# Two memory chains worked by halves of the heads, in a set TensorE order, with full row tiles for the last 64 channels

## The chip, the cores and the metric

The kernel runs on one core of one Trainium2 chip. The metric is the device time of one execution in microseconds (us). The page of a profile names the engines PE (TensorE), PEld (TensorE's weight loads), DVE (VectorE), ACT (ScalarE), POOL (GpSimd) and SP (SyncE).

## The reference, cut to what matters

The output is a gate between two attention layers, and the kernel returns it with the gradients of eleven inputs. The change touches layer B alone, which carries a memory of 8 tokens through 64 segments of 32 tokens, with 32 heads of 128:

```python
mem = mem0                                    # 8 x 576
for s in range(64):
    h = concatenate([mem, x[32*s : 32*s+32]]) # 40 tokens
    q, k, v = h @ Wq, h @ Wk, h @ Wv          # 32 heads x 128
    p = softmax(q k^T * scale + mask)
    o = (p v) @ Wo
    mem = o[:8]                               # into the next segment
    outs.append(o[8:])
```

The kernel does what depends on x alone in bulk, and only the 8 memory tokens in order: a forward chain of 64 segments, and for the gradients a backward chain from the last segment to the first. Each segment waits for the one before.

## The kernel before

The 8 x 576 memory is held as columns: four blocks of 128 channels and one of 64 (`NKT` = 5). A projection is five row blocks times four groups of four heads; the groups stand side by side in the array (`tp`), so four matmuls of 512 columns run at once. The fifth block has 64 rows only. One segment of the forward chain:

```python
S = psum.tile([P, 512], F32, name="c_S", bufs=1)
self.mm(S[:, :], lhsT=self.identB[:, :], rhs=self.maskC..., start=True, stop=False)
for wi, w in enumerate("qkv"):
    for r in range(2):                        # halves of the heads
        for kt in range(NKT):
            for g in range(4):
                wap, rows = self.w_nat(w, kt, c * 512, (c + 1) * 512)   # 64 rows where kt == 4
                self.mm(pb[32 * g:32 * g + 32, :], lhsT=mT[rows, kt, s * MEM:s * MEM + 32],
                        rhs=wap, start=(kt == 0), stop=(kt == NKT - 1), tp=(rows.start, 32 * g))
        self.evac(tm[w][:, r, :], pb[:, :])
    ...                                       # 8 transposes, one copy for all heads
...                                           # 16 score matmuls
self.busy(pf, 2, mE[:, 0:512])
nc.scalar.activation(ET[:, :], S[:, :], ACT.Exp, scale=SCALEB)     # all heads at once
...                                           # row sums, outputs
self.busy(pf, 4, ET[:, :])
...                                           # reciprocal, scaling, two transposes
self.busy(pf, 4, oc[:]...)
...                                           # 96 matmuls with Wo
self.rows_to_columns(...)                     # the result to columns: the tail
```

`busy` is a fill-in matmul: its result goes nowhere, and it is there to keep TensorE's clock up.

```python
def busy(self, pf, n, rhs):
    for _ in range(n):
        self.mm(pf[0:32, 0:w], lhsT=self.identB[:, 0:32], rhs=rhs)
```

The backward segment begins with the probabilities, computed again:

```python
nc.scalar.activation(ET[:, 256:512], S[:, :], ACT.Exp, scale=SCALEB)
for x in range(2):
    self.mm(Sg[:, 1, :], lhsT=self.onesPB[:, :], rhs=ET[:, 256 * x:256 * x + 256], ...)
nc.vector.reciprocal(rlb[:, :], Sg[:, 1, :])  # 128 x 256
self.evac(cc[:], pt[:])                       # q, k and probabilities, transposed
...                                           # dO = gradient @ Wo^T, 40 matmuls
self.busy(self.pf, 2, dO[:, 0]); self.busy(self.pf, 1, dO[:, 1])
...                                           # dO^T, dP, dS, each for all heads
project(3, "v", ...); project(2, "k"); project(1, "q")   # 288 matmuls into one accumulator
self.rows_to_columns(...)
```

## Time and profile before

| | us |
|---|---|
| median of 3 runs | 9754.34 |
| up to the first forward copy | 3997 |
| forward chain, 62 segments | 1112 |
| between the chains | 1639 |
| backward chain, 63 segments | 1149 |
| after it | 1842 |

The chain rows run from the first to the last of the copies that end a segment (`c_mT`, `d_gT`); their lines and those of single segments are in the prediction below. The period between two such copies is the measure: it repeats 62 and 63 times in one trace.

### The profile page before, as it was taken

Reading aid. Unit: us, or ns where it says so; the run is one execution under the profiler, and the core shown is the slowest. Engines: PE = TensorE matmul, PEld = TensorE weight load, DVE = VectorE, ACT = ScalarE, POOL = GpSimd, SP = SyncE. Lnnn points to the kernel's source line nnn. Section 1 sums busy time; section 2 is a strip of 40 time slices with the busy share of each in tenths; the row PEclk is TensorE's granted clock in tenths of the full one; section 3 lists DMA queues with packets and bytes.
Section 4 is the critical chain, followed back from the end, with each engine's and each line's share of the span. In section 5 each row is a group of like instructions: output and inputs, shape, how many; then the busy total and the mean of one; then the engine's idle time right before and its main releaser. Section 6 shows DMA issues by size and latency. Waiting matters only on the chain. (4 is left out here: it accounts for less than half of the span.)

```text
span 9738.9 us, 211095 instructions
## 1 busy us (share of the span) xinstructions
PE 9052.5 (93%) x91222; PEld 4192.6 (43%) x91222; DVE 4369.3 (45%) x6082; ACT 3748.2 (38%) x6962; POOL 1261.4 (13%) x2887
## 2 busy tenths in 40 slices
PE   7999999999999898899998888887999989998899
PEld 2222222222223344445455555554666655554444
DVE  4889888889887343122223333332222211113100
ACT  3878778778876233111113222221111111112000
POOL 3000000000000233000002222221000001112000
PEclk9999999999999899899997777777999987776999
DMA  2000000000000555211115444444222256666444
GB/s 80 1 5 5 1 5 5 1 5 5 1 1 27 211 232 214 88 48 51 48 49 196 155 157 156 155 161 164 77 78 80 77 176 185 190 186 210 166 150 145
DMA packets 550264, 961.40 MB, mean 99 GB/s; under 512 B 183433, under 2 KB 361746, under 8 KB 529170
## 3 DMA queue, kind: packets, MB, share of 16 engines
q1 hardware_dynamic: 484002, 697.41, 22.3%
q0 software_dynamic: 64016, 249.18, 6.7%
q8 instruction: 713, 11.68, 0.5%
q14 instruction: 221, 1.81, 0.1%
q10 hardware_dynamic: 1312, 1.33, 0.0%
HBM read 543.67 MB, written 404.03 MB: 97 GB/s over the span
## 5 line engine op out<-in xcount | busy, mean ns | idle before, releaser
L1128 DVE TENSOR_TENSOR a_U<-a_d,a_E 128x1024 bf16<-128x1024 f32 x2048 | 2472.6, 1223 | 295.2 <-ACT a_E L1123 224.0
L1123 ACT ACTIVATE a_E<-a_s 128x512 bf16<-128x512 f32 x4096 | 2237.7, 595 | 556.7 <-PE a_s L78 471.8
L78 PE MATMUL a_s<-a_qaug,a_kmask 128*128 128x512 bf16 x2048 | 700.1, 385 | 54.7 <-ACT a_tk L1205 24.5
L78 PE MATMUL a_s<-a_kmask,a_qaug 128*128 128x512 bf16 x2048 | 697.1, 383 | 25.9 <-ACT a_E L1123 9.6
L78 PE MATMUL w_acc<-w_col,w_h 128*128 128x512 bf16 (+1 forms) x2400 | 525.5, 380 | 11.0 <-DMA w_col<-dqx 11.0
L78 PEld LDWEIGHTS <-d_g 128*32 128x32 bf16 x18432 | 498.9, 97 | 26.2 <-DVE d_g L740 9.8
L62 DVE CAST p_tok<-p_pb 128x512 bf16<-128x512 f32 x384 | 265.2, 691 | 319.1 <-PE p_pb L78 319.1
L78 PE MATMUL a_d<-a_doT,a_vaugT 32*128 32x512 bf16 x2048 | 399.0, 386 | 0.0
L78 PE MATMUL a_d<-a_vaugT,a_doaT 32*128 32x512 bf16 x2048 | 398.0, 385 | 0.0
L78 PEld LDWEIGHTS <-w_h 128*128 128x128 bf16 (+1 forms) x2400 | 237.3, 100 | 299.4 <-issue 33.7
L64 ACT COPY p_em<-p_tr 128x512 bf16<-128x512 bf16 x384 | 224.7, 585 | 358.7 <-PE p_tr L83 358.5
L1215 POOL TENSOR_TENSOR a_otok<-a_tk,a_rl 128x144 bf16<-128x144 f32 x64 | 27.4, 428 | 2514.1 <-DVE a_rl L1214 2514.1
L78 PEld LDWEIGHTS <-a_vaugT 32*128 32x128 bf16 x2048 | 96.1, 91 | 569.0 <-issue 569.0
L78 PEld LDWEIGHTS <-a_doaT 32*128 32x128 bf16 x2048 | 96.3, 91 | 537.9 <-issue 537.5
L64 ACT CAST c_tm<-c_pb 128x512 bf16<-128x512 f32 x192 | 112.3, 585 | 540.7 <-PE c_pb L78 540.7
L78 PEld LDWEIGHTS <-c_mT 128*32 128x32 bf16 (+1 forms) x7680 | 166.7, 94 | 328.9 <-issue 209.6
L824 ACT ACTIVATE g_dt<-x_p 128x512 bf16<-128x512 f32 x256 | 142.7, 600 | 355.2 <-DMA dvx<-g_dt 185.4
L62 DVE CAST w_o<-w_acc 128x512 bf16<-128x512 f32 (+1 forms) x60 | 41.4, 690 | 491.7 <-PE w_acc L78 475.4
L78 PEld LDWEIGHTS <-a_kmask 128*128 128x128 bf16 x2048 | 124.9, 97 | 311.2 <-issue 303.1
L78 PEld LDWEIGHTS <-p_xT 128*128 128x128 bf16 (+1 forms) x1920 | 155.0, 97 | 218.4 <-issue 88.4
L345 DVE CAST d_ws<-d_pw 96x128 bf16<-96x128 f32 x64 | 18.4, 287 | 497.9 <-ACT d_ws L344 497.9
L78 PE MATMUL x_b<-WTq,g_dqe 128*128 128x512 bf16 (+1 forms) x1024 | 200.7, 360 | 42.9 <-DMA g_dqe<-dqe 42.9
(485 smaller groups left out, 15029.5 us busy)
## 6 DMA issues: line engine op xcount, KB each, us to landing
xt_k<-p_tok SPq DMA_DIRECT2D x16, 1024.0 KB, 3.9
xe_k<-p_em POOLq DMA_DIRECT2D x16, 1024.0 KB, 5.3
xs_k<-p_seg POOLq DMA_DIRECT2D x64, 256.0 KB, 3.6
xt_v<-p_tok SPq DMA_DIRECT2D x16, 1024.0 KB, 4.0
xe_v<-p_em POOLq DMA_DIRECT2D x16, 1024.0 KB, 5.8
xs_v<-p_seg POOLq DMA_DIRECT2D x64, 256.0 KB, 3.7
xt_q<-p_tok SPq DMA_DIRECT2D x16, 1024.0 KB, 4.2
xe_q<-p_em POOLq DMA_DIRECT2D x16, 1024.0 KB, 5.8
```

Source lines behind the costliest of these rows:

```text
L62: nc.vector.tensor_copy(out, in_)
L64: nc.scalar.copy(out, in_)
L78: self.follow(self.nc.tensor.matmul(out, lhsT, rhs, start=start, stop=stop, tile_position=tp, skip_group_check=True))
L345: nc.vector.tensor_copy(ws[0:96, 0:128], pw[0:96, 0:128])
L824: nc.scalar.mul(dt[:, g], pk[:], sc)
L1123: nc.scalar.activation(ex[:, j, :], s[:, :], ACT.Exp, scale=SCALEA)
L1128: nc.vector.tensor_tensor(out=u[:], in0=d[:], in1=ex[:], op=ALU.mult)
L1215: nc.gpsimd.tensor_tensor(out=osl, in0=v[:, :, :, o0:o0 + DA], in1=rl[:].to_broadcast([P, 4, 2, DA]), op=ALU.mult)
```

## The change

Its intent is to shorten a segment in three ways: full 128-row tiles (zeros beside the last 64 channels), so that TensorE never changes to the 64-row shape; every step between projections done for 16 heads at a time, so that VectorE and ScalarE work on one half while TensorE works on the other; and an order for TensorE written out by hand and held (`chain`), with useful work where fill-in matmuls stood. The 1/sum of the softmax is also kept from the forward chain, and a backward segment needs eight matmuls fewer besides the fill-in ones: two row sums, and six of those that build dP. Cut to its core:

```diff
-        mT = keep.tile([P, NKT, NSEG * MEM + 32], BF16, name="c_mT")
+        mT = keep.tile([P, NKT + 1, NSEG * MEM + 32], BF16, name="c_mT")
+        self.chain = True
...
+                        elif w == "v":
+                            blk, rhs = 4 + r, self.Wv5[:, g * 512:(g + 1) * 512]
+                        else:
+                            blk, rhs = 4 + (w == "k"), self.Wqk5[:, c * 512:(c + 1) * 512]
+                        self.mm(pb[32 * g:32 * g + 32, :], lhsT=mT[:, blk, s * MEM:s * MEM + 32], rhs=rhs,
+                                start=(kt == 0), stop=(kt == NKT - 1), tp=(0, 32 * g))
...
+            project("q", 0, "v")
+            project("q", 1, "s")
+            project("k", 0, "v")
             for r in range(2):
+                self.evac(half(0, r), compact(columns("q", r)), use="vs"[r])
+            project("k", 1, "s")
+            project("v", 0, "v")
...                                           # k transposes
+            project("v", 1, "s", 0)           # three of its five row blocks
...                                           # mask and scores
+            for r in range(2):
+                nc.scalar.activation(ET[:, :, rs], S[:, :, rs], ACT.Exp, scale=SCALEB)
+            project("v", 1, "s", 1)           # the other two, while ScalarE works
-            self.busy(pf, 4, ET[:, :])
-            self.busy(pf, 4, oc[:].rearrange("p r n -> p (r n)"))
+            output(0)
...
+            self.busy(pf, 1, ET[:, 0, :])
+            output(1)
+            out_columns(0)
...
+            out_project(0, 8)
+            out_columns(1)
+            out_project(8, 32)
...                                           # backward
+            rlb = L["rlb"] = sp.tile([P, 256], F32, name="d_rlb", bufs=2)
+            nc.sync.dma_start(rlb[:, :], self.RL_m[s].partition_broadcast(P))
-            nc.vector.reciprocal(rlb[:, :], Sg[:, 1, :])
+            def weight_gradients(r):
+                dP[r] = psum.tile([P, 2, P], F32, name="d_S", bufs=1)
...
+            gradient_rows(0)
+            own_exps(L)
+            gradient_rows(1)
+            gradient_columns(0)
+            fill(1, dO[0][:, 0:192])
+            gradient_columns(1)
+            compact_gradient(0)
+            weight_gradients(0)
+            compact_gradient(1)
+            score_gradients(0)
...
+            project(3, "v", 16, 32)
+            project(2, "k", 0, 32)
+            project(1, "q", 0, 32)
+            if nxt:
+                own_scores(nxt)               # of the next segment, under the tail
```

## The prediction

> **What bounds the kernel now.** I read the page first, then stretches of 100 us with the granted clock, then the two chains instruction by instruction.
>
> ```profile
> PE 9052.5 (93%) x91222; PEld 4192.6 (43%) x91222; DVE 4369.3 (45%) x6082; ACT 3748.2 (38%) x6962; POOL 1261.4 (13%) x2887
> PE   7999999999999898899998888887999989998899
> PEclk9999999999999899899997777777999987776999
> ...
> 4500.00:4600.00 100.00, 99.67 (x1652) 49.31 (x1644) 23.59 (x55) 19.93 (x39) 3.00 (x11) 1.00 0.15 45
> 7300.00:7400.00 100.00, 98.56 (x2249) 69.79 (x2251) 28.69 (x59) 14.18 (x35) 0.62 (x5) 1.00 0.27 85
> ...
> L352 DVE CAST c_mT<-c_tr x63: 198/200/201, 3997.4 to 5109.5; 128x40 bf16<-128x40 f32 x63
> L352 DVE CAST d_gT<-d_tr x64: 198/199/200, 6748.5 to 7897.0; 128x40 bf16<-128x40 f32 x64
> ```
>
> TensorE is busy everywhere (first number of a stretch), the others below half. The last two lines are the copies that end one segment of the forward and of the backward memory chain. So the forward chain takes (5109.5 - 3997.4)/62 = 17.94 us a segment, the backward one (7897.0 - 6748.5)/63 = 18.23 us, together some 2,320 of 9,754 us. A segment needs the one before it, so each microsecond of one counts 63 or 64 times. The 99% busy there mean little: part is filler, and matmuls overlap. One forward segment, in order of time:
>
> ```profile
> 4499.79 1.05 PE L78 MATMUL c_pb<-Wq,c_mT 128*32 128x512 bf16 x16
> 4500.77 0.40 PE L78 MATMUL c_pb<-Wqk,c_mT 64*32 64x512 bf16 x4
> 4501.09 1.05 PE L78 MATMUL c_pb<-Wq,c_mT 128*32 128x512 bf16 x16
> 4502.07 0.40 PE L78 MATMUL c_pb<-Wqk,c_mT 64*32 64x512 bf16 x4
> 4502.40 0.40 PE L83 MATMUL c_tr<-identB,c_tm 128*128 128x128 bf16 x4
> 4502.73 0.60 PE L78 MATMUL c_pb<-Wk,c_mT 128*32 128x512 bf16 x5
> ...
> 4513.30 2.82 PE L78 MATMUL c_S<-Wo,c_mE 128*32 128x192 bf16 x96
> 4515.95 0.59 PE L78 MATMUL c_pf<-c_mE,identB 128*32 128x512 bf16 x2
> 4516.16 0.21 ACT L344 CAST c_ws<-c_S 96x64 bf16<-96x64 f32 x1 [4.76 <-PE c_S L78]
> 4516.40 0.29 DVE L345 CAST c_ws<-c_S 96x128 bf16<-96x128 f32 x1 [3.16 <-ACT c_ws L344]
> 4517.47 0.20 DVE L352 CAST c_mT<-c_tr 128x40 bf16<-128x40 f32 x1 [0.78 <-PE c_tr L78]
> ```
>
> and the start of a backward one:
>
> ```profile
> 7314.69 1.76 DVE L669 RECIPROCAL d_rlb<-d_g 128x256 f32<-128x256 f32 x1 [1.09 <-PE d_g L78]
> 7316.37 0.50 DVE L62 COPY d_cc<-d_tr 128x768 bf16<-128x768 bf16 x1
> 7316.78 0.68 DVE L62 CAST d_dO<-d_pb 128x512 bf16<-128x512 f32 x1
> 7317.51 0.81 PE L78 MATMUL d_pf<-d_dO,identB 128*32 128x512 bf16 x3 [0.31 <-DVE d_dO L62]
> ```
>
> Four matmuls of 32 columns by 512 run side by side, so 16 are four groups. Starts tell the cost: the 16 take 0.98 us to the next kind, the 4 with 64 rows 0.32. At 0.216 us a group that is 0.11 us over, at each change of tile shape; 4 transposes take 0.33 = 4 x 0.056 + 0.11. In the backward piece the reciprocal and the copy behind it hold VectorE until the cast of dO starts late, and TensorE waits.
>
> **What the Trainium skill says.** "TensorEngine Tiling (Array Packing)", Key Properties: changing the tiling mode drains TensorE. The trace agrees, 0.11 us each. "TensorE: Matmul & The Clock Gate", "Wait - 56ns, not 53.3ns?": 215.7 ns for 512 columns, 55.6 for 128; the groups above agree. Same page, Part 1: the clock is judged in free-running windows of 3.41 us and is full or half. The clock records agree: lengths are multiples of 3.41, values 1.0 or 0.5. I summed streamed columns (at the page's 2.4 GHz, half in the low state) per such window over the whole trace: every drop followed a window that streamed at most 45% of the time; none followed a fuller one. "PSUM - Partial Sum Buffer", bank collisions: accesses by two engines to one bank are kept apart. In the tail above, ScalarE's cast ends at 4516.37 and VectorE's begins at 4516.40.
>
> **The change, forward.** Drain 0.11, group of 512 0.216, transpose 0.056, all from above. Before, 4499.79 to 4517.72: projections with their transposes up to the scores 10.01; scores to the first output matmul 1.45; outputs to Wo 2.05; Wo 2.57; tail 1.85; sum 17.93.
>
> After: (1) The last 64 channels become full 128-row tiles (zeros beside them), so the 64-row shape is gone, and nine shape changes net with it (six into it, three out of it to another projection); the fixed order does 8 transposes at a time and no longer cuts a projection after five matmuls (5 take 0.53, a broken group). Up to the scores: 28 groups 6.05, 16 transposes 0.90, 5 drains 0.55 = 7.50. (2) The mask's matmul moves here (0.22, from the tail), 16 score matmuls at 0.025 = 0.40, then the last two groups of v (0.43) with two drains (0.22) cover the exponential, instead of fillers: 1.27. The two half exponentials (about 0.38 each, as the backward 128x256 one) suffice: the first ends 0.65 after the scores, the cover lasts 0.65. (3) Outputs by halves: 0.39 each, v transposes 0.33, a small filler 0.22, five transposes with drain 0.39 = 1.72. Then Wo's first part waits for its columns: second output, reciprocal 0.17, copy 0.22 (128 wide, from 0.291 for 256 and 0.424 for 512) and hand-over end 0.21 later: 1.93. Fillers of 4 x 512 and 4 x 256 leave; what they covered is shorter. (4) Wo 2.57, one transpose and two drains in it: 2.85. (5) Tail: 0.29 until VectorE sees the sum, 0.35 for 192 columns (0.287 for 128 plus 1.05 ns each), 0.03, 0.22 for 64, 0.06, last matmul 0.19, 0.04, copy 0.20, 0.05 = 1.43. The third filler and the mask no longer stand before the last copies.
>
> Sum 7.50 + 1.27 + 1.93 + 2.85 + 1.43 = 14.98, against 17.94: 2.96 x 63 = 186 us.
>
> **The change, backward.** Before (7313.65 on): 4.60 to the transposes of dO, 3.09 to the first Wv matmul, 2.12 to the long run, that run (240 matmuls) 6.80, tail 1.79; 18.40 here, 18.23 on average. After: the 1/sum comes from the forward chain by DMA, so the 1.76 us reciprocal, its two row sums and their drains go; scores of the next segment and the copy of q and k move into the tail. Start: ten groups 2.16, two transposes 0.11, three drains 0.33 = 2.60. Middle, by halves, to the first Wv matmul: this is a VectorE chain, dO cast to second transposes at 3.34, dO^T products to 4.25, dS of half 0 to 4.67; the second half's gradients share its one PSUM bank and so start only at 4.72. With half-size operations at 0.29 (VectorE) and 0.27 (ScalarE) the Wv matmuls begin near 5.24: 2.64. Wv's 48 in three pieces (1.28), with keys, queries, score transposes and eight drains between: 2.48. Long run 6.80, unchanged. Tail 1.43 as above; the moved scores (0.55) fit under the casts. Sum 15.95: 2.28 x 64 = 146 us.
>
> Other parts: the 1/sum rows written once, some 2 us; loading v first and q last helps little, because the first segment's own mE (a 31.6 us wait in the trace) stays behind the same weight loads. Sum: 186 + 146 - 2 = 330. Hand schedules miss waits, so I take 10 off: 9754 - 320 = 9434, say 9435.
>
> **Rivals.** (A) The clock falls. Fillers stand there to keep it up; of 13 forward per segment 3 stay, backward only one short one. Against: adding up columns, the thinnest 3.41 us window I find is about 54% forward (7.45 to 10.86) and 53% backward (2.6 to 6.0), above every drop seen, but not by much. A stall of 0.5 us more there would cross 45%, and half a clock for one window in five costs 1 to 2 us a segment: then 9550 to 9650. (B) The waits take the fillers' place: fillers cost nothing where TensorE waited anyway. For it: the long backward middle is VectorE's, and 128 wide operations cost 0.29 where 256 wide cost 0.42, so halves mean more VectorE time. Then only drains and the reciprocal come out, about 1.5 + 1.2 us a segment: some 170 us, 9580. Against: forward VectorE is a fifth busy, and most of its gain is removed TensorE time. (C) The order is better than I think, with waits overlapping: 9350.
>
> **Range and chances.** B halfway gives the upper end, C the lower: 9345 to 9545. Two per cent is 9559. Faster by over 2% 0.92, within 2% 0.07, slower 0.01.
>
> **What would show it.** The c_mT copies should come 15.0 us apart, the d_gT copies 15.95; no matmul with 64*32 in either chain; a forward projection of 20 in 1.08; after scores no wait over 0.15 before the outputs; granted clock 1.00 from 4000 to 4950 and through the backward chain; the one large wait in a backward segment before the second half's d_S matmuls, some 0.5 us. Stages outside the chains should keep their length within 5 us each. I am wrong if the clock row shows 9 or less inside a chain, if a segment waits for the small rl_m loads, or if the d_gT copies stay above 17 us.

## More of the kernel before

Of the groups that write the tile `d_pf`, in the kernel before (count, then duration in ns as minimum, median and maximum):

```profile
L78 PE MATMUL d_pf<-d_dO,identB x384: 376/379/634, 6694.9 to 7884.7; 128*32 128x512 bf16 x192
L78 PE MATMUL d_pf<-d_g,identB x192: 378/379/390, 6747.0 to 7896.2; 128*32 128x512 bf16 x192
L78 PE MATMUL d_pf<-d_dOc,identB x128: 272/282/421, 6736.2 to 7886.1; 128*32 128x256 bf16 x128
```

704 over 64 segments is 11 a segment; forward it is 13. They count as busy time like any other matmul.

## The result, and the profile after

The changed kernel took 9412.99 us (median of 4 runs, 9407.91 to 9418.01), the kernel before 9754.98 in the same rounds. The ratio is 0.9647, 95% interval 0.9631 to 0.9664, so it is faster by 3.5%. A ratio is the mean time of one kernel's fast runs over that of the other's of the same rounds, so it is not quite the ratio of the medians that are quoted. 9413 was predicted as 9435, in a range of 9345 to 9545.

Busy times and TensorE's clock in 40 slices, from the page of the changed kernel, then the two closing copies:

```profile
PE 8638.8 (92%) x89432; PEld 4097.2 (44%) x89432; DVE 4330.9 (46%) x6561; ACT 3805.1 (40%) x7316; POOL 1282.8 (14%) x3014
PEclk9999999999999899799997777777999977776999
...
L394 DVE CAST c_mT<-c_tr x63: 206/208/209, 3999.9 to 4920.5; 128x48 bf16<-128x48 f32 x63
L394 DVE CAST d_gT<-d_tr x64: 206/208/209, 6561.9 to 7572.1; 128x48 bf16<-128x48 f32 x64
```

The shares on the first line barely moved, and they would not have told the result. The copies do: (4920.5 - 3999.9)/62 = 14.85 us forward where it was 17.94, and (7572.1 - 6561.9)/63 = 16.03 backward where it was 18.23. That is 1112.2 to 920.6 and 1148.5 to 1010.2 us, together 329.9. The part up to the first copy grew by 2.5 us, that between the chains by 2.4, the rest by 0.5. So the 324.4 us between the two traces come from the chains alone. (The trace before is of an execution of 9740.96 us, below its median; hence 324 and not 342.)

Where a forward segment's time is now (start, duration, engine, what, count):

```profile
4490.19 1.05 PE L78 MATMUL c_pb<-Wq,c_mT 128*32 128x512 bf16 x16 [0.30 <-DVE c_mT L394]
...
4497.69 0.39 PE L78 MATMUL c_S<-maskC,identB 128*128 128x512 bf16 x1
...
4498.40 0.61 PE L78 MATMUL c_pb<-Wv,c_mT 128*32 128x512 bf16 x8
4498.95 0.20 PE L78 MATMUL c_o<-onesB,c_ET 128*128 128x1 bf16 x2
...
4500.77 0.84 PE L78 MATMUL c_S<-Wo,c_mE 128*32 128x192 bf16 x24
...
4505.05 1.05 PE L78 MATMUL c_pb<-Wq,c_mT 128*32 128x512 bf16 x16 [0.30 <-DVE c_mT L394]
```

7.50 us up to the mask, 1.26 to the first sum (no wait before it: the two groups of v just cover the exponential), 1.82 to Wo, and 4.28 for Wo and the tail. Split where the prediction splits them (at 4503.63, the end of the last Wo matmul's turn), that is 2.86 and 1.42. Backward, the waits and the long run:

```profile
6802.45 0.40 PE L83 MATMUL d_tr<-identB,d_dO 128*128 128x128 bf16 x4 [0.23 <-ACT d_dO L64]
...
6803.82 0.22 PE L78 MATMUL d_S<-d_g,d_mE 128*128 128x128 bf16 x1 [0.30 <-DVE d_dS L783]
...
6806.73 1.50 PE L78 MATMUL d_pw<-WTcv,d_g 128*32 128x192 bf16 x48
6808.06 2.81 PE L78 MATMUL d_pw<-WTck,d_g 128*32 128x192 bf16 x96
6810.70 2.81 PE L78 MATMUL d_pw<-WTcq,d_g 128*32 128x192 bf16 x96
6813.45 0.28 PE L78 MATMUL d_g<-maskD,identB 128*128 128x256 bf16 x1
```

This segment takes 15.74 us, as most do (the median). The mean is 16.03, because of a stretch of slow segments in the second half of the chain, up to 17.4 us. What TensorE waited for in equal stretches of the two halves of the chain, 6600 to 7050 and 7050 to 7500 (us in total, times, longest), first half above:

```profile
PE d_pb L78 <- DVE d_gT L394: 8.4, 28, 0.3
PE d_S L78 <- DVE d_dS L783: 8.3, 28, 0.3
PE d_tr L83 <- ACT d_dO L64: 6.5, 28, 0.2
```

```profile
PE d_pw L78 <- issue: 8.9, 21, 0.7
PE d_pb L78 <- DVE d_gT L394: 8.4, 28, 0.3
```

"issue" means that no semaphore explains the wait. Such a wait lies in the middle of the long run, where operands and accumulator are the same before and after:

```profile
7305.44 1.41 PE L78 MATMUL d_pw<-WTck,d_g 128*32 128x192 bf16 x45
7307.56 1.58 PE L78 MATMUL d_pw<-WTck,d_g 128*32 128x192 bf16 x51 [0.72 <-issue]
```

I counted TensorE's instructions (weight loads, matmuls and semaphore events) from the start of the program. A gap is taken here from the start of one matmul to the start of the next. In the first ten kernels, all of the some 240 gaps over 0.3 us inside the backward chain's long runs lie at one and the same count modulo 256 of their kernel (193 or 194), and so they do in the later ones. (In e12_before_pad_nofill the count reads 233, as 217 matmul records are missing from that trace before the chain.) And each of the 240 ends 1.13 to 1.64 us after a 16 KB packet has landed in a DMA queue that the page calls "instruction". Between 6600 and 7500 that queue moved 168 packets of 16 KB; 21,573 matmuls, 21,570 weight loads and 114 semaphore events of TensorE start there, which is 169.0 times 256. So the theory that came out of the trace: TensorE's instructions arrive in pieces of 256, and where it runs through a piece in 3.5 us (the fastest here) the next one can be late. A segment has 772 instructions, 3 x 256 + 4. The edge moves by 4 a segment, so that in about 26 of 64 segments it falls badly. In sum the gaps at that count (less the 0.03 us that usually lies between two such starts) come to 16.3 us in this chain. In the kernel before they were 8.8, a part of it ordinary waits that fell on the count: a segment there has 808 instructions, so its edge moves by 40 a segment, and slow segments lie scattered.

### The profile page after: what moved, and what is told of

It reads as the page before. It is cut to its first block, busy times and chain, and to the rows that moved or that the text cites. A ratio compares the mean times of both kernels' runs of the same rounds, so it can differ in the third digit from the quotient of the medians.

```text
span 9414.5 us, 208637 instructions
## 1 busy us (share of the span) xinstructions
PE 8638.8 (92%) x89432; PEld 4097.2 (44%) x89432; DVE 4330.9 (46%) x6561; ACT 3805.1 (40%) x7316; POOL 1282.8 (14%) x3014
## 5 line engine op out<-in xcount | busy, mean ns | idle before, releaser
L62 DVE CAST c_tm<-c_pb 128x512 bf16<-128x512 f32 x192 | 132.9, 692 | 313.5 <-PE c_pb L78 309.1
L78 PEld LDWEIGHTS <-c_mT 128*32 128x32 bf16 x7680 | 187.9, 96 | 190.9 <-DVE c_mT L394 25.4
```

Of the source, the lines that this page charges most:

```text
L62: nc.vector.tensor_copy(out, in_)
L78: self.follow(self.nc.tensor.matmul(out, lhsT, rhs, start=start, stop=stop, tile_position=tp, skip_group_check=True))
```

## The experiments

Theory at the start: the gain is the sum of removed drains (padding), of useful work in place of waits and fill-in matmuls (order), and of hidden VectorE and ScalarE work (halves and the kept 1/sum). Rivals: the fixed order alone does it; padding is worthless; the fill-in matmuls hold the clock, and it falls without them; what is taken out comes back as waits. A "drain" is the 0.11 us that a change of tile shape costs in the prediction's reading. Twelve kernels ran; all gave correct results. "Typical" is the median period, "stalls" the sum of the gaps at the 256 count in the backward chain (from one trace of each kernel: four kernels with 772 instructions a segment, changed, e1, e2 and e10, lie between 11.4 and 24.3, so a few us there mean nothing), "half clock" the number of stretches at half clock in the forward and in the backward chain by the clock records (most are one window of 3.41 us).

| kernel | us | ratio to before | forward typical (mean) | backward typical (mean) | half clock | stalls |
|---|---|---|---|---|---|---|
| before | 9754.98 | 1 | 17.93 (17.94) | 18.19 (18.23) | 0, 0 | 8.8 |
| changed | 9412.99 | 0.9647 | 14.85 (14.85) | 15.74 (16.03) | 0, 0 | 16.3 |
| e1_rows64 | 9497.28 | 0.9736 | 15.84 (15.84) | 16.17 (16.39) | 0, 0 | 24.3 |
| e2_free_order | 9407.52 | 0.9642 | 14.63 (14.63) | 15.83 (16.04) | 0, 0 | 11.4 |
| e5_before_pad | 9714.31 | 0.9962 | 17.05 (17.06) | 18.42 (18.36) | 0, 0 | 10.7 |
| e8_whole | 9504.65 | 0.9745 | 15.21 (15.22) | 16.60 (17.06) | 0, 21 | 2.9 |
| e3_before_nofill | 9674.50 (one run) | | 17.48 (17.88) | 16.71 (17.06) | 15, 12 | 7.1 |
| e4_after_nofill | 9431.82 | 0.9668 | 14.87 (14.88) | 16.34 (16.34) | 0, 0 | 31.0 |
| e6_recip | 9452.16 | 0.9689 | 14.85 (14.85) | 16.43 (16.65) | 0, 1 | 8.7 |
| e7_bank | 9434.05 | 0.9667 | 14.85 (14.85) | 15.83 (16.27) | 0, 0 | 44.7 |
| e10_shift | 9415.02 | 0.9656 | 14.85 (14.85) | 15.77 (16.08) | 0, 0 | 18.0 |
| e11_nofill_shift | 9397.46 | 0.9636 | 14.87 (14.87) | 15.74 (15.80) | 0, 0 | 4.1 |
| e9s_combined_shift | 9354.79 | 0.9594 | 14.65 (14.66) | 15.20 (15.30) | 0, 0 | 3.2 |
| e12_before_pad_nofill | 9617.53 | 0.9866 | 16.59 (17.06) | 16.67 (17.06) | 19, 16 | 6.9 |

Where stalls hit most segments, even the median is no longer that of an undisturbed segment. There I give the fastest period that recurs.

### e1_rows64: padding undone

```diff
-   blk, rhs = 4 + r, self.Wv5[:, g * 512:(g + 1) * 512]
+   blk, rhs = 4 + r, self.Wv5[64 * r:64 * r + 64, g * 512:(g + 1) * 512]
...
+   rows = slice(0, P) if kt < 4 else slice(64 * (blk - 4), 64 * (blk - 4) + 64)
-   self.mm(pb[32 * g:32 * g + 32, :], lhsT=mT[:, blk, s * MEM:s * MEM + 32], rhs=rhs, ..., tp=(0, 32 * g))
+   self.mm(pb[32 * g:32 * g + 32, :], lhsT=mT[rows, blk, s * MEM:s * MEM + 32], rhs=rhs, ..., tp=(rows.start, 32 * g))
```

> The changed kernel with the 64-row tiles back for the last 64 channels in both memory chains. Theory (each switch between the 128-row and the 64-row form drains TensorE for about 0.11 us; 9 of them come back in the forward segment, 2 on the path of the backward one): forward segment 14.85 to about 15.85 us, backward median 15.74 to about 15.96, total about 9488. Rival (padding is worth nothing, the halves did it): both periods and the total as in the changed kernel, about 9413.

Forward 15.84: 0.995 us for nine changes of shape is 0.111 each. Backward the recurring period is 15.96, 0.22 more, again as expected. Within 0.01 us a segment, padding is worth its drains.

### e5_before_pad: padding alone

```diff
-   mT = keep.tile([P, NKT, NSEG * MEM + 32], BF16, name="c_mT")
+   mT = keep.tile([P, NKT + 1, NSEG * MEM + 32], BF16, name="c_mT")
-   self.mm(..., lhsT=mT[rows, kt, s * MEM:s * MEM + 32], rhs=wap, ..., tp=(rows.start, 32 * g))
+   self.mm(..., lhsT=mT[:, blk, s * MEM:s * MEM + 32], rhs=rhs, ..., tp=(0, 32 * g))
+   nc.scalar.copy(ws[0:96, 256:320], pw[0:96, 128:192])
```

> The kernel before with the padded full row tiles alone, no halves and no fixed order. Theory (padding is worth its drains): forward segment 17.94 to about 17.1 us (about 9 drains of 0.11 taken away, 0.2 given back for a further copy in the tail), backward unchanged to 0.2 shorter, total about 9715 (9695 to 9735). Rival (padding gives nothing by itself): 9754.

9714 us where 9715 was expected. Forward lost 0.88. Backward was a small miss: the mean grew by 0.13 instead of staying or shrinking. The trace says where: in the kernel before, undisturbed segments take 18.03 and 18.18 us in turn, because the copy of q and k (`evac`) goes to ScalarE in one and to VectorE in the next. Padding made the first kind shorter, 17.96, and the second longer, 18.42. Why the second kind lost is not shown.

### e2_free_order: the fixed order off

```diff
-        self.chain = True
+        self.chain = False
```

> The changed kernel with the hand-set TensorE order switched off in both chains, the scheduler choosing. Theory (the halves and the source order do it, the fixed order by itself is nearly irrelevant): forward about 14.63 us, since the scheduler puts the fill-in matmul for the clock into the tail wait, backward within 0.1 of 15.74; total about 9399. Rival (the fixed order is the gain): the segments go back toward 17 us and the total to 9500 or more.

9407.5, and the ratio's interval (0.9626 to 0.9657) overlaps the changed kernel's. The scheduler keeps almost the same order, since it follows the source; it moves the mask's matmul into the tail (forward 14.63) and one small product backward (typical 15.83). The mechanism that holds the order has no measurable worth here, so the gain that is left to order must come from writing the steps in that order in the source. No run undoes that alone.

### e8_whole: halves undone

```diff
-            for r in range(2):
-                nc.scalar.activation(ET[:, :, rs], S[:, :, rs], ACT.Exp, scale=SCALEB)
+            nc.scalar.activation(ET[:, :, :], S[:, :, :], ACT.Exp, scale=SCALEB)
...                                           # in the same way the outputs, dO^T, dP, dS, keys, queries
-            score_gradients(0)
...
+            nc.vector.scalar_tensor_tensor(out=dS[:, 1, :], in0=dPw[:, 1, :], ...)
+            nc.vector.scalar_tensor_tensor(out=dS[:, 0, :], in0=dPw[:, 0, :], ...)
```

> The changed kernel with the halves undone in both chains: every step works on all heads at once, the order still fixed and the tiles still padded. Theory (halves only hide VectorE and ScalarE work that the fixed order does not cover already): forward 14.85 to about 15.1 us, backward 15.74 to about 16.5; total about 9479. Rival (halves are the main part of the change): forward 16 or more, backward 17 or more, total above 9560.

The typical periods came close (15.21 and 16.60), but the total of 9505 is 26 us over. The stretch from 6800 to 7500 tells why: its last columns are granted clock, DMA share and GB/s. Below it are the two largest waits from 6600 to 7500.

```profile
6800.00:7500.00 700.00, 621.47 (x15703) 483.72 (x15703) 148.46 (x410) 120.00 (x288) 11.15 (x82) 0.97 0.31 91
...
PE d_pw L78 <- DVE d_g L844: 40.2, 52, 0.8
PE d_tr L83 <- DVE d_g L823: 29.9, 52, 0.6
```

The waits for VectorE that the halves had hidden are back, 0.8 and 0.6 us a segment, and with them TensorE streams too little in some windows. There were 21 stretches at half clock in the backward chain, 71.7 us in all. Half of that is 36 us; mean less the recurring period of 16.52, times 63, is 34. Summed as in the prediction, with matmuls that run side by side counted once, the windows before these falls stream 29 to 34% of the time; the thinnest of the changed kernel's backward chain streams 46%. So the halves are worth 0.8 us a backward segment in hidden work, and another 0.5 because they keep the clock. I had expected only the first.

### e3_before_nofill and e4_after_nofill: no fill-in matmuls

```diff
-        for _ in range(n):
+        for _ in range(0):                    # in busy(), in the kernel before and in the changed one
```

> The kernel before with every fill-in matmul (those that only keep the clock up) removed. Theory (before, the fillers were needed: without them TensorE streams too little in the windows of the chains, and the clock falls in parts of both): granted clock below 1.00 in stretches of both chains and 100 to 150 us slower, 9850 to 9905. Rival (the fillers were never needed): clock stays 1.00 and each segment about 0.2 to 0.4 us shorter, 9705 to 9730.

> The changed kernel with every fill-in matmul removed. Theory (the denser segment holds the clock by its own work): clock stays 1.00 in both chains, forward 14.85 to about 14.68 us (one filler of 0.17), backward unchanged; total about 9403. Rival (my rival A: the clock falls, since windows stream too little): clock below 1.00 in stretches of a chain, and slower than 9413 by 20 us or more.

The totals of both theories missed, and these runs taught most about the change. For the kernel before, forward and backward stretches:

```profile
4100.00:4900.00 800.00, 713.93 (x12806) 375.61 (x12805) 186.29 (x448) 151.16 (x312) 23.02 (x89) 0.98 0.17 50
6800.00:7500.00 700.00, 641.26 (x16081) 488.97 (x16076) 215.39 (x431) 109.94 (x266) 5.10 (x41) 0.98 0.28 84
```

The clock did fall, as expected (15 and 12 stretches; a forward segment with one takes 19.13 us in place of 17.48). Yet the kernel became 81 us faster, not 100 to 150 slower. That is a single execution, but the mean periods of its trace give 78 of them: 4 us forward and 74 backward. Without its eleven fill-in matmuls a backward segment takes 16.7 us instead of 18.2. So most of them had been standing before work that was ready, and backward holding the clock was worth less than they cost; forward the two nearly cancel. In the changed kernel the clock stays at full speed without them, as expected there, and forward they cost nothing (14.87 against 14.85): the three left stand in waits. So my rival A falls, and so does the expected 0.17.

That kernel was nevertheless 19 us slower than the changed one. The trace puts it in the backward chain alone, where no undisturbed segment changed (15.74 recurs), but the stalls rose from 16.3 to 31.0 us. Two instructions fewer a segment means 770: the edge of the pieces moves by 2 a segment, so the chain stays longer in the bad place, which it entered almost at once: 39 segments have such a gap, where it was 21.

### e6_recip: the reciprocal back

```diff
-   nc.sync.dma_start(rlb[:, :], self.RL_m[s].partition_broadcast(P))
+   for x in range(2):
+       self.mm(pl[:, :], lhsT=self.onesPB[:, :], rhs=L["ET"][:, x, :], start=(x == 0), stop=(x == 1))
+   nc.vector.reciprocal(L["rlb"][:, :], pl[:, :])
```

> The changed kernel with the row sums and the 128x256 reciprocal of the probabilities taken back into the backward chain, in place of the 1/sum that the forward pass stored. Theory (the reciprocal sits on the path between the exponentials and the first products of the start): backward median 15.74 to about 16.4 us, forward unchanged, total about 9458. Rival (VectorE has room there and the reciprocal hides): backward within 0.15, total 9413 to 9423.

16.43 typical, so the kept 1/sum is worth 0.69 us a backward segment and 39 us in all. That is less than the 1.75 us that the reciprocal takes in this trace, so VectorE has room for the rest of it; that the halves make this room is not shown, as it was not taken back in the kernel before.

### e7_bank: a PSUM bank for the second half

A bank is a part of PSUM, the memory that matmuls write to.

```diff
-   dP[r] = psum.tile([P, 2, P], F32, name="d_S", bufs=1)
+   dP[r] = psum.tile([P, 2, P], F32, name="d_S", bufs=1) if r == 0 else psum.tile([P, 2, P], F32, name="d_pb", bufs=2)
```

> The changed kernel with the second half's score gradients in a PSUM bank of their own instead of the bank that the first half is still being read from. Theory (the 0.5 us between the first half's and the second half's matmuls is a wait for the bank, and on the path): that wait is gone, backward median 15.74 to about 15.54, total about 9400. Rival (the gap only moves: what follows waits for VectorE's chain all the same): backward within 0.05, total 9413.

The wait on `d_dS` is gone, and the recurring period is 15.52, 0.22 less, as the theory said. But the kernel is not faster. Its median is 9434 (runs from 9415 to 9440; the ratio's interval, 0.9651 to 0.9683, still overlaps the changed kernel's), and the stalls of its trace rose to 44.7 us. The unexplained waits from 6600 to 7550, where d_dS no longer appears:

```profile
PE d_pw L78 <- issue: 31.7, 42, 1.7
```

A true gain on the path was paid back at another limit. That a tighter segment has less slack for late instructions is my reading; what made the stalls so much longer is not shown. By its total alone, this run would have spoken for the rival.

### e10_shift and e11_nofill_shift: moving the edge

```diff
         self.chain = True
         L = load(NSEG - 1)
+        pd = psum.tile([P, 192], F32, name="d_pw", bufs=1)
+        for _ in range(64):                   # 55 in e11_nofill_shift
+            self.mm(pd[0:32, 0:32], lhsT=self.identB[:, 0:32], rhs=self.identB[:, 0:32])
```

> The changed kernel with 64 small unneeded matmuls (with their weight loads, 128 instructions) on TensorE just before the backward memory chain. Theory (the stalls of TensorE inside the backward chain are waits for its own instructions, which arrive in pieces of 256; a segment has 772 of them, so the piece's edge moves by 4 a segment and lies badly in about 26 of 64 segments): the late segments move by 32, from segments 33 to 58 to segments 1 to 27, and every stall still ends on the same count modulo 256; typical segment still 15.74, total within 10 us of the changed kernel, near 9415. Rival (transfers that come at that time, or the place in memory of those segments, delay them): the late segments stay at 33 to 58.

> The changed kernel without fill-in matmuls, as in the earlier run, with 55 small unneeded matmuls (110 instructions) just before the backward memory chain. A segment now has 770 instructions, so the edge moves by only 2 a segment, 126 in the chain, and the shift starts it at the place from which the whole chain passes through the good half. Theory (instruction arrival): TensorE's stalls of 0.3 us or more in the chain fall from 31 us to under 4 in sum, backward mean 16.34 to about 15.8, median 15.74, total 9432 to about 9400. Rival (the stalls have to do with missing fill-in matmuls, by clock or otherwise): mean stays at 16.2 or more, total 9430.

Matmuls of no use, executed once before the chain, moved the slow stretch. In the changed kernel 1.0 us of the stalls lay in segments 1 to 30 and 15.3 in the rest; in e10_shift it was 16.4 (segments 5 to 30) and 1.5. What TensorE waited for in the second half of that chain, 7050 to 7500, to be set against the 8.9 us there above:

```profile
PE d_S L78 <- DVE d_dS L786: 8.5, 29, 0.3
PE d_pb L78 <- DVE d_gT L394: 8.4, 28, 0.3
PE d_tr L83 <- ACT d_dO L64: 6.7, 29, 0.2
PE d_pw L78 <- issue: 0.4, 2, 0.3
```

In e11_nofill_shift, with 770 instructions a segment, 55 such matmuls led the whole chain through the good half: stalls 31.0 to 4.1 us, mean 16.34 to 15.80, time 9431.82 to 9397.46 (intervals of the ratio 0.9654 to 0.9683 and 0.9623 to 0.9650). The unexplained waits from 6600 to 7500, first in e4_after_nofill, then here:

```profile
PE d_pw L78 <- issue: 18.0, 40, 0.9
...
PE d_pw L78 <- issue: 1.1, 4, 0.3
```

Adding instructions made the kernel faster by 34 us. A transfer at a fixed time or a fixed place in memory does not explain that; the count of instructions does. e8_whole fits too: with 768 instructions a segment, 3 x 256, its edge does not move, and its stalls are 2.9 us. What stays open is why a piece is sometimes asked for late: where the changed kernel runs through a piece in under 4 us, the packet's transfer starts 0.15 to 1.55 us after TensorE has passed the last edge. An estimate from these traces: that start, then 0.9 to 1.8 us for the transfer (168 packets), then at least 1.13 us before TensorE goes on, make 2.2 us at best and 4.5 at worst, against the 3.5 us of a fast piece.

### e12_before_pad_nofill: two edits at once

The diffs of e5_before_pad and e3_before_nofill together.

> The kernel before with the padded full row tiles and without any fill-in matmul: neither halves nor the new order. It splits what the two edits gave one by one (padding 0.88 us of the forward segment, missing fillers 0.46 of its typical one). Theory (the two add up, and what is left to the changed kernel is the new order and the halves): typical forward segment about 16.6 us, with the half-clock episodes that the kernel before showed without fillers still there, so a mean of about 17.0; backward median about 16.9, mean about 17.2; total about 9635. Rival (they overlap, since both shorten what VectorE waits for): forward 16.9 or more typical, total 9660 or more.

Forward 16.59, the sum of the two to 0.01, and 17.06 in the mean with 19 stretches at half clock. (Backward 16.67 came below the 16.9 expected, and the total, 9618, below 9635.) That closes the account of the forward segment, typical periods: 17.93, less 0.88 for padding = 17.05, less 0.46 for fill-in matmuls = 16.59, less 1.38 for the new order of the source, with what came with it = 15.21 (e8_whole), less 0.36 for halves = 14.85. The 1.38 is what is left over between two kernels; no run takes it apart.

### e9s_combined_shift: what the runs pointed to

```diff
-        for _ in range(n):                    # busy: none
+        for _ in range(0):
+   S = mask()                                # the mask's matmul in the tail of the segment before
...
+   dP[r] = ... if r == 0 else psum.tile([P, 2, P], F32, name="d_pb", bufs=2)
...
             gradient_rows(0)
-            own_exps(L)
             gradient_rows(1)
+            own_exps(L)                       # its copy on VectorE instead of ScalarE
...
+        for _ in range(55): ...               # as in e11_nofill_shift
```

> A candidate to beat both: the changed kernel without fill-in matmuls, with the mask's matmul in the forward tail, the second half's score gradients in a bank of their own, the next segment's own exponentials after both halves' gradient rows (their copy on VectorE), and the same 55 small matmuls ahead of the backward chain that put the edges of the instruction pieces in the good half. Theory: forward about 14.63 us, backward median about 15.25 to 15.5 and mean within 0.1 of it, total about 9365 (9350 to 9380). Rival (without the shift's effect: the tighter backward segment runs into instruction arrival in most segments as the kernel with the own bank did): backward mean 16 or more, total 9395 or more.

The closing copies of this kernel:

```profile
L400 DVE CAST c_mT<-c_tr x63: 207/208/209, 3997.2 to 4905.9; 128x48 bf16<-128x48 f32 x63
L400 DVE CAST d_gT<-d_tr x64: 207/208/209, 6546.0 to 7509.6; 128x48 bf16<-128x48 f32 x64
```

9354.79 us, ratio 0.9594 (0.9581 to 0.9607): 58 us less than the changed kernel, which is 0.19 x 62 = 12 forward and 0.74 x 63 = 47 backward, from the means. The clock stayed full, and stalls came to 3.2 us. The typical backward period, 15.20, is 0.54 below that of e11_nofill_shift; the own bank, which had gained nothing by itself, can account for 0.22 of that, and the rest would be that of the moved exponentials; this run does not separate the two.

## Why the prediction was right

Its forward steps held one by one: 7.50, 1.27, 1.93, 2.85 and 1.43 were predicted; 7.50, 1.26, 1.82, 2.86 and 1.42 came. Its total of 186 us forward came as 192 to 195 (62 periods in the trace, 63 by its own multiplier). "No matmul with 64*32", a projection of 20 in 1.08 (1.09: 4505.05 to 4506.14), no wait after the scores, full clock in both chains, and other stages within 5 us each all held.

Backward the steps were 2.60, 2.64, 2.48, 6.80 and 1.43; in the typical segment above they are 2.60, 2.61, 2.49, 6.72 and 1.32, so 15.74 where 15.95 was predicted. The one large wait it named is there (`d_dS`; 0.51 us from start to start), and e7_bank showed that 0.22 of it is on the path.

Three things it did not have right, though its total was:

1. "Hand schedules miss waits, so I take 10 off." The missed wait is none of the schedule's. It is the late arrival of TensorE's own instructions: 16.3 us, shown by e10_shift and e11_nofill_shift. It stands against a typical backward segment that was 0.2 us shorter than predicted, and the two nearly cancel in the mean (16.03 against 15.95). That the backward mean and the total came so close is therefore partly luck.
2. The backward gain was put down to the start of a segment, 4.60 to 2.60, with the reciprocal and its sums as the parts named. e6_recip gives these 0.69 us. e3_before_nofill shows that the fill-in matmuls alone cost the kernel before 1.48 of the 2.44 us by which the typical segment fell. My rival B ("fillers cost nothing where TensorE waited anyway") was true of the three that are left, and false of the eleven backward ones. These parts overlap and do not add up as the forward ones do. The piece shown in the prediction, with the copy of q and k on VectorE ahead of the cast of dO, is also only every second segment; in the others that copy runs on ScalarE, and they are 0.15 us shorter.
3. Rival A took the fill-in matmuls for what holds the clock, with 54% and 53% as the thinnest windows. Summed in the same way, the thinnest windows of the changed kernel stream 57% forward and 46% backward, and 54% and 45% without any fill-in matmul: less margin backward than predicted, yet the clock held in both. It is the halves that keep the windows full backward: with whole heads and the order still set by hand, the clock fell 21 times.

## What to carry to other kernels

A fill-in matmul for the clock can be on the path like any other matmul, and should be tested by taking it out: here a denser segment held the clock by itself, and in the backward chain of the kernel before the fillers cost more than the half clock would have. In a long unrolled run of short matmuls, look at whether the waits that nothing explains lie a multiple of 256 instructions apart; if they do, the number of instructions per iteration, and a few added ones ahead of it, move or remove them. And judge a step by the period of an undisturbed segment as well as by the total, as one limit can hide the gain at another.

## What the Trainium skill lacked or had wrong

- "Runtime: NRT & Kernel Launch", Instruction fetch mechanics, has instructions fetched in 16 KiB blocks of 256, which these traces agree with (16 KB packets, gaps at one count modulo 256). It calls the fetch hidden, because the sequencer dispatches more slowly than it is refilled. Here it was not always hidden: a block ran in 3.5 us at the fastest, and the gaps at the block edges came to 16.3 us of the backward chain, 44.7 in e7_bank and 4.1 in e11_nofill_shift. The page gives TensorE room for 2048 instructions, but also speaks of two lines of 16 KiB; the first does not show here, as a packet that ended such a wait had landed only 1.13 to 1.64 us before TensorE went on.
- "TensorE: Matmul & The Clock Gate", Why this matters for your kernels, advises against gaps of over some 3 us (the same page, A second HAM failure mode, tells of a kernel whose short idle times came often enough to bring the clock down). In e8_whole the profile lists no TensorE wait longer than 0.8 us from 6600 to 7500, and the clock fell 21 times in that chain. The page gives no level of activity; where I added up the streamed columns, each fall followed a window that streamed at most 45% of the time in the kernel before, the changed one, e3_before_nofill, e8_whole and e9s_combined_shift. In e4_after_nofill and e6_recip one fall each, some 95 us after the start, came after a window of 73% by that count, which stays unexplained. And 45% is no level at which the clock must fall: inside the chains, windows down to 36% were followed by full clock.
- "TensorEngine Tiling (Array Packing)", Key Properties, says that a change of tiling mode drains TensorE, but not for how long: 0.111 us, from nine of them in e1_rows64.
